# A fused recurrence and rational-activation kernel: last unit's denominator sum by accumulating DMA, and a new order table

## The chip, the cores and the metric

The kernel runs on one core of a Trainium2 chip. The metric is the device time of one execution in microseconds; the time before is 221.01 us, the median of 5 runs (220.28 to 221.08). A profile of one further execution shows every engine's instructions: PE (matrix multiply), DVE (elementwise), ACT (activations), POOL (here small copies and the issue of DMAs that cast or accumulate), SP (issue of plain DMAs). All times inside an execution are counted from its first instruction.

## The reference

Two parts follow each other. The first is a gated linear recurrence per batch and head (4 x 8, 768 steps, 48 channels); the second feeds the result, as 3072 tokens of 384 channels, through a projection to 2048, a rational function, and a projection back to 384.

```python
f = 1.0 / (1.0 + np.exp(-f_logit))
for t in range(S):
    state = f[:, :, t, :, None] * state + np.einsum('bhd,bhe->bhde', k[:, :, t], v[:, :, t])
    y[:, :, t] = np.einsum('bhd,bhde->bhe', q[:, :, t], state)
x = np.ascontiguousarray(attn_out.transpose(0, 2, 1, 3)).reshape(B * S, H * D)
h = x @ w_in
h2 = h * h
P = a[0] + a[1] * h + a[2] * h2 + a[3] * h2 * h
Q = 1.0 + np.abs(b[0]) * np.abs(h) + np.abs(b[1]) * h2
g = P / (Q + 1e-06)
out = g @ w_out
```

## The kernel before

The work is cut into 12 units: unit n is batch n mod 4 and one third of the sequence, 256 tokens, held as two chunks of 128. The recurrence is done in chunked form, with a state carried from third to third of a batch, so unit n needs unit n−4. Each unit goes through some 70 *steps*. A step is a small Python function that records one instruction, or a group on one engine.

The whole program is one table, `ORDER`, a text of 829 steps such as `h 3 4 8 @2`: name, unit, further numbers (first and last of 16 blocks of 128 hidden channels, or of 4 head pairs, or a chunk), and `@` with the PSUM slot that it takes. Scheduling is manual (`tc.manual_schedule()`): the program is recorded in the table's order, so each engine runs its own steps in that order, strictly one after another; waits between engines, and waits for a buffer or a slot to come free, are put in automatically. There are four PSUM slots of one buffer each. A step that waits holds up everything behind it on its engine, and for SP and POOL everything behind it in their DMA queues.

Steps that matter here, by engine:

- SP: `ld n f|k|q` load a unit's gate logits, keys and queries in f32 (L200, 384 KB; unit 0 in two halves), in three rotating buffers; `ld 0 v` too. `ab_` loads the coefficients `b` and `a`, each spread over 128 partitions (L228, L230). `so` stores a unit's output (L590).
- POOL: `ca`, `cb` make triangular masks and the identity; `wi` loads `w_in` with a cast (L216), `wo` `w_out` (L220), `ld n v` the values (L200), `vm` copies some of their columns (L388). `ta` (L559) and `zd` (L525) are DMAs within on-chip memory that add 512 KB of bf16 onto another tile.
- ACT: `ef`, `ls` make the log of the gate (L308, L313); `A n 1|0` exponentials of its running sum (L332); `ae` those of the sum over the unit (L461); `ye` evicts the recurrence's output, scaled (L456); `hy` evicts the projection (L488), `sa` its square (L496); `ln` and `lz` take the logarithm of the denominator (L516 from PSUM, L532 from on-chip memory); `ex` its exponential with sign turned, that is the reciprocal (L540); `oe`, `oc` evict the output. `b1_` issues a DMA that loads `b` onto one partition (L224), and `rg` loads two registers from coefficients made of it.
- DVE: `cz`, `cc` fill constants; `hv` writes a word of `w_in`'s tile, so that `wi` can't start earlier; `fa 0` and `fa 1` make coefficients from `b` on one and on 128 partitions (L277 to L287), `fb` scales `a` with them (L296); `xa n 1|0` multiply keys or queries by `A` (L337); `Te` copies transposes out of PSUM (L356); `mk` masks the scores (L377); `st` forms the new state (L465); `sq` squares (L492), `ab` takes the absolute value (L500), `p1`, `p2`, `pm` and `tv` build the numerator (L545, L550, L555, L563), `gm` multiplies by the reciprocal (L568).
- PE: `cs` running sums (L323), `T` transposes (L348), `sc` scores (L369), `sv` and `id` the state (L413, L424), `yb` the recurrence's output (L394), `h` first projection (L474), `u` a sum by two identity matmuls (L508), `o` second projection (L581).

The denominator of a unit is `z = |h| + h2`, with the coefficients folded into scales. It is summed in one of two ways. Either PE adds the two tiles into PSUM, and the logarithm reads PSUM, in steps of 4 blocks:

```python
for x, src in ((0, s["h2"]), (1, s["z"])):
    for m in range(m0, m1, 2):
        nc.tensor.matmul(t[:, m - m0:m - m0 + 2, :].rearrange("p m t -> p (m t)"), ident,
                         fl(src, m, m + 2), start=(x == 0), stop=(x == 1))
```

or `zd` adds them by DMA, and `lz` reads the sum from on-chip memory in one step of 8 blocks:

```python
nc.gpsimd.dma_start(out=fl(s["z"], m0, m1), in_=fl(s["h2"], m0, m1), accum_op=ALU.add)
```

Units 0 and 1 use PE throughout, units 2 to 10 use `zd` for one half or both, unit 11 uses PE for all of its four quarters. At the start of the table, DVE's steps are `cz 0; cc; cz 1; fa 0; cz 3; cz 2`, the four `xa 0` with `hv 0` after two of them, `Te 0` in two halves, `st 0 0`, two `mk 0`, `xa 1 1; st 0 1; fa 1; xa 1 0; fb; Te 1`. PE's in that stretch are `yb 0; id 1 0; h 0 0 4; T 1; h 0 4 8; sc 1 0; sc 1 1`.

Of the kernel before, what the change touches and what calls it, by code (L numbers as in the profile page):

```python
# [19 lines left out]
b1_; cz 0; cb; ca; ld 0 f 2 4; ld 0 f 0 2; ld 0 q 2 4; cc; ld 0 k 2 4; cz 1; ld 0 k 0 2; fa 0  # L20
ef 0 2 4; ld 0 q 0 2; ls 0 2 4; ef 0 0 2; cs 0 2 4 @0; ld 0 v; cz 3; ls 0 0 2; A 0 1 2 4; ld 1 f
cs 0 0 2 @1; cz 2; A 0 0 2 4; A 0 1 0 2; xa 0 1 2 4; A 0 0 0 2; ld 1 k; xa 0 0 2 4; rg; hv 0
xa 0 1 0 2; T 0 2 4 @1; wi 0 4; ld 1 q; xa 0 0 0 2; id 0 0 @0; Te 0 2 4; T 0 0 2 @2; vc 0; ab_
wi 4 8; vm 0 0 s; Te 0 0 2; ae 0; sc 0 0 @2; sc 0 1 @1; sv 0; ef 1; ld 2 f; ld 1 v; ls 1; st 0 0
wi 8 16; mk 0 1; id 0 1; vm 0 1 s; cs 1 @3; mk 0 0; A 1 1; yb 0 0 4 @2; A 1 0; xa 1 1; st 0 1
id 1 0 @3; ye 0; fa 1; ld 2 q; h 0 0 4 @2; ld 2 k; xa 1 0; fb; T 1 @0; hy 0 0 4; h 0 4 8 @1; ae 1
Te 1; sc 1 0 @0; hy 0 4 8; sc 1 1 @2; mk 1 0; ld 3 f; ef 2; sv 1; vm 1 0; sq 0 0 8; ls 2; ld 2 v
cs 2 @0; ab 0 0 8; ld 3 v; mk 1 1; u 0 0 4 @1; A 2 1; vm 1 1; A 2 0; st 1 0; u 0 4 8 @2; p1 0 0 8
ln 0 0 4; id 1 1; h 0 8 12 @0; p2 0 0 8; ld 3 q; ln 0 4 8; pm 0 0 8; yb 1 0 4 @2; ex 0 0 8; xa 2 0
h 0 12 16 @1; st 1 1; ld 3 k; ye 1; tv 0 0 8; hy 0 8 12; h 1 4 8 @2; xa 2 1; hy 0 12 16; vm 2 0  # L30
id 2 0 @0; gm 0 0 8; wo 8 12; hy 1 4 8; sv 2; ld 4 f; vm 2 1; h 1 0 4 @1; sq 0 8 16; ae 2; sa 1 4 8
wo 0 4; wo 4 8; ef 3; p1 0 8 16; h 1 12 16 @2; wo 12 16; hy 1 0 4; st 2 0; ab 0 8 16; vm 3 1; id 2 1
ld 4 q; sa 1 0 4; T 2 @3; ab 1 0 8; vm 3 0; ld 4 v; st 2 1; ls 3; u 1 0 4 @1; Te 2; hy 1 12 16
cs 3 @0; pm 0 8 16; ln 1 0 4; u 0 12 16 @3; A 3 1; sc 2 0 @2; p2 0 8 16; h 1 8 12 @1; A 3 0; mk 2 0
ln 0 12 16; sc 2 1 @0; xa 3 1; u 0 8 12 @2; ld 5 f; hy 1 8 12; ld 4 k; mk 2 1; u 1 4 8 @3; ef 4
id 3 0 @1; ln 0 8 12; ab 1 8 16; yb 2 0 4 @0; xa 3 0; ls 4; sv 3; ld 5 v; p1 1 0 16; ye 2; T 3 @2
ln 1 4 8; o 0 0 0 4 @0; Te 3; ex 0 8 16; cs 4 @3; o 0 1 0 4; tv 0 8 16; h 2 0 4 @2; A 4 0; sq 1 8 16
A 4 1; o 0 1 4 8; sa 2 0 4; gm 0 8 16; h 2 4 8 @3; ld 6 f; ae 3; ld 5 q; hy 2 0 4; pm 1 8 16
o 0 1 8 12; hy 2 4 8; h 2 12 16 @2; pm 1 0 8; ex 1 0 8; st 3 0; o 0 0 4 8; p2 1 0 16; id 3 1
o 0 1 12 16; hy 2 12 16; o 0 0 8 12; st 3 1; ta 1 0 8; sa 2 4 8; xa 4 1; sc 3 0 @1; sc 3 1 @2  # L40
vm 4 1; o 0 0 12 16; ef 5; ld 7 f; mk 3 0; ld 5 k; h 2 8 12 @3; ef 6; mk 3 1; ld 6 q; oe 0 0 2 s
u 1 8 12 @1; hy 2 8 12; ab 2 0 8; yb 3 0 4 @2; xa 4 0; ls 5; u 1 12 16 @3; vm 5 1; ab 2 8 16
ln 1 8 12; vm 4 0; sq 2 8 16; T 4 @0; zd 2 0 8; ln 1 12 16; so 0 0 2; cs 5 @1; ta 1 8 16; ye 3; Te 4
u 2 12 16 @3; A 5 0; p1 2 0 16; sv 4 @0; A 5 1; sc 4 1 @2; ex 1 8 16; h 3 0 4 @1; mk 4 1; ld 6 k
p2 2 0 16; h 3 4 8 @2; hy 3 0 4; gm 1 0 8; ln 2 12 16; id 4 0; u 2 8 12 @1; ae 4; hy 3 4 8; xa 5 0
h 3 12 16 @3; ls 6; st 4 0; xa 5 1; ef 7; id 4 1; ld 8 f; h 3 8 12 @2; st 4 1; hy 3 12 16; pm 2 0 8
sv 5 @0; ln 2 8 12; sc 4 0 @3; id 5 0; ta 2 0 8; hy 3 8 12; mk 4 0; o 1 0 0 4 @1; ae 5; o 1 0 4 8
lz 2 0 8; st 5 0; cs 6 @3; ab 3 0 8; pm 2 8 16; o 1 1 0 4; A 6 0; yb 4 0 4 @2; gm 1 8 16; ta 2 8 16
A 6 1; id 5 1; o 1 1 4 8; ex 2 0 8; sq 3 0 8; o 1 0 8 12; o 1 1 8 12; p1 3 0 16; zd 3 0 8; ye 4
T 5 @3; ld 6 v; ex 2 8 16; st 5 1; h 4 0 4 @2; Te 5; ld 7 v; ld 9 f; ld 7 k; o 1 0 12 16; vm 5 0  # L50
pm 3 0 8; ld 7 q; hy 4 0 4; h 4 4 8 @3; sa 4 0 4; xa 6 0; o 1 1 12 16; ab 3 8 16; sa 4 4 8
h 4 8 12 @2; gm 2 0 8; hy 4 4 8; sq 3 8 16; h 4 12 16 @0; oe 1 0 2 s; hy 4 8 12; gm 2 8 16
o 2 0 0 4 @1; hy 4 12 16; sc 5 0 @2; xa 6 1; sc 5 1 @3; o 2 0 4 8; ls 7; mk 5 0; o 2 1 0 4; lz 3 0 8
cs 7 @0; ab 4 0 8; ld 10 f; u 3 8 12 @2; so 1 0 2; mk 5 1; A 7 1; o 2 1 4 8; ln 3 8 12; p2 3 0 16
yb 5 0 4 @3; A 7 0; sv 6 @2; ab 4 8 16; ld 8 k; ta 3 0 8; ye 5; o 2 0 8 12; pm 3 8 16; ex 3 0 8
# [12 lines left out]
sc 7 0 @2; hy 6 0 4; o 4 0 0 4 @1; mk 7 0; sa 6 0 4; o 4 1 0 4; o 4 0 4 8; mk 7 1; ex 5 8 16; T 8 @3
sq 6 8 16; yb 7 0 4 @0; ls 9; p1 6 0 16; u 6 12 16 @2; ld 10 v; ye 7; lz 5 0 8; o 4 1 4 8; ab 6 0 8
Te 8; o 4 1 8 12; h 7 4 8 @0; ln 6 12 16; pm 6 8 16; ex 5 0 8; h 7 0 4 @3; gm 5 8 16; vm 9 0  # L70
ld 10 q; zd 6 0 8; ld 10 k; o 4 0 8 12; p2 6 0 16; so 3 0 2; hy 7 4 8; o 4 0 12 16; vm 9 1; cs 9 @2
hy 7 0 4; gm 5 0 8; ta 6 8 16; sc 8 1 @0; A 9 0; o 4 1 12 16; sq 7 0 8; A 9 1; h 7 12 16 @3; mk 8 1
oe 4 0 2 s; ef 10; sc 8 0 @2; ld 11 q; sv 8 @1; pm 6 0 8; id 8 0; hy 7 12 16; u 6 8 12 @0; mk 8 0
ls 10; ta 6 0 8; h 7 8 12 @3; ae 8; ln 6 8 12; xa 9 1; cs 10 @2; hy 7 8 12; st 8 0; o 5 0 0 4 @0
ab 7 0 8; ex 6 8 16; yb 8 0 4 @3; xa 9 0; zd 7 0 8; sv 9 @1; sq 7 8 16; id 9 0; ye 8; o 5 1 0 4
p1 7 0 16; ae 9; A 10 0; o 5 1 4 8; ef 11; T 9 @3; st 9 0; ld 11 k; ab 7 8 16; A 10 1; h 8 12 16 @1
Te 9; zd 7 8 16; lz 6 0 8; h 8 8 12 @2; pm 7 8 16; hy 8 12 16; xa 10 1; o 5 0 4 8; hy 8 8 12
sc 9 1 @3; p2 7 0 16; sc 9 0 @1; o 5 1 8 12; so 4 0 2; ls 11; h 8 4 8 @2; mk 9 0; ex 6 0 8
ta 7 8 16; ld 11 v; mk 9 1; o 5 0 8 12; o 5 1 12 16; hy 8 4 8; ab 8 8 16; o 5 0 12 16; sa 8 4 8
# [565 lines left out]
```

## Time and profile before

| what | us |
|---|---|
| median of 5 runs | 221.01 |
| the profiled execution's own time | 220.79 |
| its span, first to last instruction | 219.1 |
| `hy` on ACT, 48 of 128x1024 | 49.3 |
| `ex` on ACT, 23 of 128x2048 | 44.8 |
| `lz` on ACT, 13 of 128x2048, mean 1996 ns | 25.7 |
| `ln` on ACT, 22 of 128x1024, mean 1077 ns | 23.3 |
| `u` on PE, the 74 recorded matmuls of 128x512, mean 379 ns | 23.2 |
| POOL issuing 13 `zd`, mean 1100 ns | 14.2 |
| a `zd` from issue to landing, median | 6.3 |
| a `ta` from issue to landing, median | 6.4 |

The page gives the busy time of each engine, and for a group of instructions the summed and the mean duration. Consecutive instructions of one engine overlap a little, so durations add up to somewhat more than the time that passes; where it matters, start-to-start distances in the timeline are the better measure. The time of an execution is 1.7 us longer than the span. Idle time before an instruction is shown in brackets, with what ended it.

### The profile page before, as it was taken

To read this page: it belongs to the slowest core of one execution; us is meant where nothing else is said; L and a number is where in the kernel's file an instruction comes from. 1 tells how busy PE (TensorE), PEld (TensorE's weight loads), DVE (VectorE), ACT (ScalarE), POOL (GpSimd) and SP (SyncE) were. 2 spreads that over 40 slices of the span, in tenths; PEclk is the share of its full clock that TensorE was granted. 3 is DMA by queue.
4 is the path that set the end of the run, shared out by engine and by line. 5 is a ranking of instruction groups with operands and counts; after the bars stand their busy time and mean duration, and the time that the engine had idled before them with its cause. 6 is when DMAs were issued, how large, how long until landed. Compare 5 with 4: busy or idle time off the path is not lost.

```text
span 219.1 us, 7100 instructions
## 1 busy us (share of the span) xinstructions
PE 202.4 (92%) x3106; PEld 143.4 (65%) x3120; DVE 202.9 (93%) x249; ACT 200.4 (91%) x215; POOL 78.7 (36%) x95
## 2 busy tenths in 40 slices
PE   1679699999999999999999999999999999999991
PEld 1446378567757778577668676786867776865450
DVE  4766999999999999999999999999999999999951
ACT  5563699999999999999999999999999999999980
POOL 4570529020261149362916633123423323231000
PEclk9999999999999999999999999999999999999999
DMA  6999999999899899699999999967988998999515
GB/s 154 292 199 202 225 225 212 204 210 242 211 227 240 222 208 152 126 274 191 214 246 257 213 269 203 212 129 130 191 155 156 195 203 165 187 200 190 107 45 144
DMA packets 62128, 42.86 MB, mean 196 GB/s; under 512 B 51474, under 2 KB 57362, under 8 KB 62098
## 3 DMA queue, kind: packets, MB, share of 16 engines
q0 software_dynamic: 19792, 23.14, 64.4%
q1 hardware_dynamic: 42144, 19.08, 34.5%
q8 instruction: 24, 0.39, 0.7%
q10 hardware_dynamic: 162, 0.20, 0.3%
q14 instruction: 6, 0.05, 0.1%
HBM read 25.17 MB, written 4.72 MB: 136 GB/s over the span
## 4 chain that ended last, share of the span: by engine, by line
PE 40%; ACT 29%; DVE 16%; issue 6%; DMA 4%; SPq 4%; ACTq 0%; DVEq 0%
PE hp L474 14%; PE op L581 13%; ACT qi L540 7%; ACT hy L488 6%; DMA b<-in_moe_b_dram 4%; SPq L200 4%; ACT lq L516 3%; ACT A L332 3%; ACT h L496 3%; PE u L508 3%; DVE h L492 3%; PE y L394 2%; PE tp L348 2%; ACT lq L532 2%; DVE gall L568 2%
## 5 line engine op out<-in xcount | busy, mean ns | idle before, releaser
L474 PE MATMUL hp<-xT,w_in_sb 128*128 128x256 bf16 x576 | 70.3, 276 | 0.8 <-ACT xT L456 0.3
L581 PE MATMUL op<-w_out_sb,gall 128*128 128x384 bf16 x384 | 69.9, 326 | 0.0
L474 PEld LDWEIGHTS <-w_in_sb 128*128 128x128 bf16 x576 | 56.1, 99 | 11.6 <-issue 1.4
L488 ACT CAST hy<-hp 128x1024 bf16<-128x1024 f32 x48 | 49.3, 1072 | 4.4 <-PE hp L474 4.4
L581 PEld LDWEIGHTS <-gall 128*128 128x128 bf16 x384 | 36.2, 98 | 23.4 <-DVE gall L568 1.1
L540 ACT ACTIVATE qi<-lq 128x2048 bf16<-128x2048 f32 (+1 forms) x25 | 46.8, 1899 | 0.1
L559 POOL DMA_DIRECT2D gall<-hy x21 | 20.1, 959 | 65.5 <-DVE gall L555 18.7
L388 POOL COPY vmp<-vn 128x128 bf16<-128x128 bf16 x22 | 27.4, 1257 | 15.9 <-DMA vn<-in_v_dram 12.6
L568 DVE TENSOR_TENSOR gall<-gall,qi 128x2048 bf16<-128x2048 bf16 (+1 forms) x25 | 29.5, 1178 | 1.5 <-ACT qi L540 1.3
L377 DVE TENSOR_TENSOR scm<-sc,mask 128x1024 bf16<-128x1024 f32 x24 | 28.8, 1216 | 0.6 <-PE sc L369 0.5
L555 DVE TENSOR_TENSOR gall<-gall,h 128x2048 bf16<-128x2048 bf16 (+1 forms) x25 | 29.2, 1172 | 0.0
L532 ACT ACTIVATE lq<-z 128x2048 f32<-128x2048 bf16 x13 | 25.7, 1996 | 0.0
L516 ACT ACTIVATE lq<-u 128x1024 f32<-128x1024 f32 x22 | 23.3, 1077 | 0.0
L525 POOL DMA_DIRECT2D z<-h x13 | 14.2, 1100 | 20.9 <-DVE z L500 4.7
L332 ACT ACTIVATE A<-cs 128x768 f32<-128x768 f32 (+1 forms) x26 | 19.2, 794 | 2.7 <-PE cs L323 2.6
L492 DVE TENSOR_TENSOR h<-hy 128x2048 bf16<-128x2048 bf16 (+1 forms) x18 | 20.9, 1163 | 0.0
L323 PE MATMUL cs<-lsp,Ui 128*128 128x384 bf16 (+1 forms) x39 | 11.1, 346 | 6.7 <-ACT lsp L313 6.7
L200 POOL DMA_DIRECT2D vn<-in_v_dram x11 | 12.0, 1093 | 14.7 <-issue 13.8
L500 DVE TENSOR_SCALAR z<-hy 128x2048 uint16<-128x2048 uint16 (+1 forms) x25 | 17.0, 681 | 0.0
L550 DVE TENSOR_SCALAR hy<-hy,a_sb 128x4096 bf16<-128x4096 bf16 (+2 forms) x15 | 16.8, 1126 | 0.1
L545 DVE TENSOR_SCALAR gall<-hy,a_sb 128x4096 bf16<-128x4096 bf16 (+2 forms) x15 | 16.9, 1124 | 0.0
L356 DVE COPY qkT<-tp 128x2048 bf16<-128x2048 bf16 (+1 forms) x13 | 14.8, 1135 | 1.6 <-PE tp L348 1.6
(70 smaller groups left out, 265.8 us busy)
## 6 DMA issues: line engine op xcount, KB each, us to landing
gall<-hy POOLq DMA_DIRECT2D x21, 512.0 KB, 6.4
z<-h POOLq DMA_DIRECT2D x13, 512.0 KB, 6.3
fn<-in_f_logit_dram SPq DMA_DIRECT2D x11, 384.0 KB, 8.3
kn<-in_k_dram SPq DMA_DIRECT2D x11, 384.0 KB, 6.4
qn<-in_q_dram SPq DMA_DIRECT2D x11, 384.0 KB, 10.7
out_dram<-osb SPq DMA_DIRECT2D x22, 192.0 KB, 3.7
vn<-in_v_dram POOLq DMA_DIRECT2D x11, 192.0 KB, 9.3
w_out_sb<-in_moe_w_out_dram POOLq DMA_DIRECT2D x4, 384.0 KB, 9.3
```

What stands on the lines that cost most here:

```text
L332: nc.scalar.activation(t, src, AF.Exp, scale=1.0 if x else -1.0)
L377: nc.vector.tensor_mul(t, s["sc", g].rearrange("s r a i t -> s (r a) (i t)"), mb)
L388: nc.gpsimd.tensor_copy(dst, src)
L474: nc.tensor.matmul(t[:, m - m0, :].rearrange("f (j t) -> f j t", j=UB), w_in_sb[:, kk, m * P:(m + 1) * P], s["x"][:, :, kk, :], start=(kk ...
L488: nc.scalar.copy(fl(big(s, "hy", "hy", 3), m0, m1), fl(s["hp", m0], 0, m1 - m0))
L492: nc.vector.tensor_mul(fl(big(s, "h2", "h2", 2), m0, m1), fl(s["hy"], m0, m1), fl(s["hy"], m0, m1))
L516: nc.scalar.activation(fl(s["lq", g], m0 - 8 * g, m1 - 8 * g), fl(s["u", m0], 0, m1 - m0), AF.Ln, scale=rsig2, bias=1.0 + 1e-6)
L532: nc.scalar.activation(fl(s["lq", g], m0 - 8 * g, m1 - 8 * g), fl(s["z"], m0, m1), AF.Ln, scale=rsig2, bias=1.0 + 1e-6)
L540: nc.scalar.activation(fl(s["qi", g], m0 - 8 * g, m1 - 8 * g), fl(s["lq", g], m0 - 8 * g, m1 - 8 * g), AF.Exp, scale=-1.0)
L555: nc.vector.tensor_mul(fl(s["g"], m0, m1), fl(s["g"], m0, m1), fl(s["h2"], m0, m1))
L568: nc.vector.tensor_mul(fl(s["g"], m0, m1), fl(s["g"], m0, m1), fl(s["qi", g], m0 - 8 * g, m1 - 8 * g))
L581: nc.tensor.matmul(s["op", j][:, 0:DM], s["g"][:, m, C * j:C * j + C], w_out_sb[:, m, :], start=(m == 0), stop=(m == KF - 1))
```

## The change

For the first half (blocks 0 to 8) of the last unit's denominator, `u 11 4 8`, `u 11 0 4`, `ln 11 4 8` and `ln 11 0 4` go, and `zd 11 0 8` and `lz 11 0 8` come in. All other steps stay, 827 in all, but the table is a new one: on each engine the steps stand in another order, near the former one. In PE's order the furthest step moves by 15 places (of 258), in ACT's by 19 (of 217), in DVE's by 8 (of 221), in POOL's by 8, in SP's by 6. Slots (`@`) are dealt anew as well.

Moves that stand out: `ca` before `cb`; `cz 0` behind the other `cz` and `cc`; `b1_` from the front of ACT's order to behind `ls 0 0 2`; `fa 0` from before the `xa 0` to behind all four; `hv 0` after three of them instead of two; `st 0 0` behind both `mk 0`; `fa 1` ahead of both `xa 1`; `T 1` ahead of `h 0 0 4`; `sv 0` ahead of `sc 0`; `ef 3` ahead of `A 2`; `ld 3 f`, `ld 4 f`, `ld 5 f` and `ld 7 f` earlier among the loads; `ef 9`, `ef 10` and `ef 11` earlier by 11, 16 and 19 places; `ld 8 k`, `ld 8 q` ahead of `so 0`.

The first and the last lines of the table, as a diff:

```diff
 ORDER = """
-b1_; cz 0; cb; ca; ld 0 f 2 4; ld 0 f 0 2; ld 0 q 2 4; cc; ld 0 k 2 4; cz 1; ld 0 k 0 2; fa 0
-ef 0 2 4; ld 0 q 0 2; ls 0 2 4; ef 0 0 2; cs 0 2 4 @0; ld 0 v; cz 3; ls 0 0 2; A 0 1 2 4; ld 1 f
-cs 0 0 2 @1; cz 2; A 0 0 2 4; A 0 1 0 2; xa 0 1 2 4; A 0 0 0 2; ld 1 k; xa 0 0 2 4; rg; hv 0
-xa 0 1 0 2; T 0 2 4 @1; wi 0 4; ld 1 q; xa 0 0 0 2; id 0 0 @0; Te 0 2 4; T 0 0 2 @2; vc 0; ab_
-wi 4 8; vm 0 0 s; Te 0 0 2; ae 0; sc 0 0 @2; sc 0 1 @1; sv 0; ef 1; ld 2 f; ld 1 v; ls 1; st 0 0
-wi 8 16; mk 0 1; id 0 1; vm 0 1 s; cs 1 @3; mk 0 0; A 1 1; yb 0 0 4 @2; A 1 0; xa 1 1; st 0 1
-id 1 0 @3; ye 0; fa 1; ld 2 q; h 0 0 4 @2; ld 2 k; xa 1 0; fb; T 1 @0; hy 0 0 4; h 0 4 8 @1; ae 1
-Te 1; sc 1 0 @0; hy 0 4 8; sc 1 1 @2; mk 1 0; ld 3 f; ef 2; sv 1; vm 1 0; sq 0 0 8; ls 2; ld 2 v
+cz 2; ca; ld 0 f 2 4; ld 0 f 0 2; ld 0 q 2 4; cb; cc; cz 1; ld 0 k 2 4; cz 3; ld 0 k 0 2; ef 0 2 4
+cz 0; ld 0 q 0 2; ls 0 2 4; ld 0 v; ef 0 0 2; cs 0 2 4 @0; ls 0 0 2; ld 1 f; b1_; cs 0 0 2 @1
+ld 1 q; A 0 1 2 4; A 0 0 2 4; xa 0 1 2 4; A 0 1 0 2; A 0 0 0 2; xa 0 1 0 2; ld 1 k; xa 0 0 0 2; hv 0
+xa 0 0 2 4; T 0 0 2 @1; wi 0 4; fa 0; vc 0; ab_; T 0 2 4 @0; vm 0 1 s; vm 0 0 s; Te 0 0 2; id 0 0 @2
+rg; ld 2 f; Te 0 2 4; wi 4 8; sv 0; ae 0; ef 1; sc 0 1 @0; ld 3 f; sc 0 0 @1; ls 1; mk 0 1; ld 2 k
+ld 1 v; id 1 0 @3; mk 0 0; cs 1 @0; wi 8 16; st 0 0; fa 1; A 1 0; id 0 1; yb 0 0 4 @1; A 1 1; xa 1 0
+ye 0; xa 1 1; ld 2 q; st 0 1; T 1 @1; fb; h 0 0 4 @2; Te 1; ld 4 f; sc 1 0 @1; hy 0 0 4; h 0 4 8 @0
+mk 1 0; ef 2; sc 1 1 @1; ae 1; hy 0 4 8; mk 1 1; ls 2; sq 0 0 8; vm 1 1; cs 2 @1; vm 1 0; ef 3; sv 1
...
-sq 11 0 8; o 9 1 0 4; hy 11 8 12; o 9 0 4 8; p1 11 0 8; ex 10 0 8; o 9 1 4 8; gm 9 8 16; u 11 4 8 @2
-pm 11 0 8; o 9 0 8 12; oe 8 0 2 s; o 9 1 8 12; hy 11 12 16; p1 11 8 12; so 8 0 2; o 9 0 12 16
-p2 11 0 8; lz 10 8 16; o 9 1 12 16; gm 10 0 8; ta 11 0 8; u 11 0 4 @3; sq 11 12 16; o 10 0 0 4 @1
-ln 11 4 8; ab 11 12 16; o 10 1 0 4; sq 11 8 12; ex 10 8 16; p1 11 12 16; o 10 1 4 8; ab 11 8 12
-u 11 12 16 @2; p2 11 8 12; p2 11 12 16; ln 11 0 4; o 10 0 4 8; pm 11 8 12; oe 9 0 2 s; gm 10 8 16
...
+gm 8 8 16; ta 10 0 8; h 11 8 12 @3; lz 10 0 8; ab 11 0 8; o 8 1 8 12; sq 11 0 8; o 8 1 12 16
+ex 9 8 16; o 8 0 8 12; gm 9 0 8; zd 11 0 8; o 8 0 12 16; pm 10 8 16; o 9 0 0 4 @1; oe 8 0 2 s
+h 11 12 16 @0; ex 10 0 8; p1 11 0 8; ta 10 8 16; so 8 0 2; gm 9 8 16; o 9 0 4 8; o 9 1 0 4
+hy 11 12 16; p2 11 0 8; o 9 1 4 8; gm 10 0 8; lz 10 8 16; o 9 1 8 12; o 9 0 8 12; pm 11 0 8
+o 9 1 12 16; hy 11 8 12; p1 11 12 16; o 10 0 0 4 @0; ta 11 0 8; sq 11 12 16; ex 10 8 16; o 10 0 4 8
+ab 11 8 12; o 10 1 0 4; ab 11 12 16; p1 11 8 12; o 10 1 4 8; p2 11 12 16; lz 11 0 8; o 9 0 12 16
+sq 11 8 12; gm 10 8 16; u 11 12 16 @3; u 11 8 12 @2; oe 9 0 2 s; p2 11 8 12; pm 11 12 16; ex 11 0 8
...
```

Between them every line of the table differs in the same manner: steps exchanged with neighbours, none added or taken out.

## The prediction

> **What bounds the kernel now.** First the page's busy times and the windows: where is there idle time to win?
>
> ```profile
> PE 202.4 (92%) x3106; PEld 143.4 (65%) x3120; DVE 202.9 (93%) x249; ACT 200.4 (91%) x215; POOL 78.7 (36%) x95
> ...
> 0.00:15.00 15.00, 7.26 (x102) 5.06 (x102) 9.68 (x36) 8.35 (x16) 8.62 (x23) 1.00 0.96 217
> 15.00:30.00 15.00, 12.27 (x221) 8.40 (x226) 11.96 (x23) 9.31 (x13) 4.39 (x7) 1.00 1.30 211
> 30.00:120.00 90.00, 88.65 (x1481) 64.22 (x1488) 89.69 (x95) 89.71 (x99) 38.59 (x35) 1.00 1.09 215
> 120.00:205.00 85.00, 84.70 (x1261) 60.94 (x1263) 84.91 (x89) 84.98 (x81) 27.11 (x32) 1.00 0.97 187
> 205.00:219.10 14.10, 9.50 (x54) 4.83 (x52) 6.69 (x10) 8.06 (x10) 0.00 (x0) 0.98 0.32 84
> ```
>
> Columns of a window: length, busy us of PE, PEld, DVE, ACT, POOL, granted clock, DMA share, GB/s. From 30 to 205 us DVE and ACT are idle 0.4 and 0.3 us of 175: no order can win much there, and neither engine's work changes. Idle time lies ahead of 30 us (ACT 12.3, DVE 8.4) and behind 205. So a shift of the moment at which the three engines become full goes nearly whole into the time. What sets that moment shows the DVE timeline:
>
> ```profile
> 15.50 0.96 DVE L337 TENSOR_TENSOR qkp<-kn,A 128x768 bf16<-128x768 f32 x1 [0.43 <-ACT A L332]
> 16.37 0.55 DVE L465 TENSOR_TENSOR state<-sv,alast 128x384 bf16<-128x384 f32 x1
> 18.20 0.17 DVE L277 TENSOR_SCALAR bm<-b 128x2 uint32<-128x2 uint32 x1 [1.28 <-DMA b<-in_moe_b_dram]
> ...
> 19.35 0.96 DVE L337 TENSOR_TENSOR qkp<-qn,A 128x768 bf16<-128x768 f32 x1
> 20.23 0.74 DVE L296 TENSOR_SCALAR a_sb<-a_sb,sig 128x3 f32<-128x3 f32 x3
> 21.49 1.23 DVE L356 COPY qkT<-tp 128x2048 bf16<-128x2048 bf16 x1 [0.53 <-PE tp L348]
> ```
>
> `fa 1` (L277 to L285) waits for the broadcast load of `b`; behind it stand `xa 1 0`, `T 1`, `Te 1`. Two steps, `xa 1 1` and `st 0 1`, run before that wait. PE meanwhile does `h 0 0 4`:
>
> ```profile
> 17.55 2.72 PE L474 MATMUL hp<-xT,w_in_sb 128*128 128x256 bf16 x12 [0.31 <-ACT xT L456]
> 20.37 1.08 PE L348 MATMUL tp<-ident,qkp 128*128 128x128 bf16 x16
> 21.29 1.48 PE L474 MATMUL hp<-xT,w_in_sb 128*128 128x256 bf16 x12
> ```
>
> The first twelve matmuls of `h` start 0.214 us apart, the next twelve 0.109; the first `T` (7.43) starts its transposes 0.107 apart, `T 1` 0.056. PE runs at half speed until about 20.3, with a granted clock of 1.00 in these windows, so that column doesn't show it.
>
> Last the end of the chain of waits:
>
> ```profile
> 205.46 1.02 PE u L508 x4
> ...
> 206.52 6.87 PE op L581 x40
> ...
> 213.41 0.33 ACT osb L604
> ```
>
> **The change at the start of the program.** Times below go by start-to-start distances in the timeline.
>
> *The wait for b moves ahead of more work.* In the new order `fa 1` stands before both `xa 1`, and `T 1` before `h 0 0 4` on PE. Let L be the landing of `b`. From L: `fa 1` 1.15 (18.20 to 19.35); two `xa` of 0.87, 1.75; `T 1` on a PE idle since `yb 0` (about 16.7), hence slow, 16 x 0.107 and 0.15 to drain, 1.86 — ends L+4.8. `h 0 0 4`, 12 x 0.214 = 2.57, ends L+7.3. `sc 1 0`, 0.3, then `h 0 4 8` at full speed 12 x 0.109 and 0.15, ends L+9.1; `sc 1 1` 0.25; `mk 1 1` 1.13, ends L+10.5 (`mk 1 0` lies in the shadow of `h 0 4 8`). Behind it DVE is full: `sq` 1.13, `ab` 0.60, `p1` 0.72, `st` 0.47: L+13.5. Before, DVE has done the same twelve steps at 28.6 (`p2 0 0 8` starts at 28.64). So DVE is late by **L − 15.1**. ACT agrees: it waits from `ye 0` (about 17) for `h 0 0 4` and for `u`.
>
> *Where L goes.* Before, the load is issued at 9.62 and lands at 18.18. Of its 128 packets of 8 bytes 120 start between 13.84 and 15.87, the last eight, one DMA engine's share, between 17.40 and 17.69; that engine carried an instruction fetch of 0.94 us at 16.04. What holds the SP queue (q1) up is w_in from POOL (q0): q1 moves 821 packets in 9 to 10 us, and once q0 has begun
>
> ```profile
> q0 software_dynamic: 150, 0.13, 93.4%
> q1 hardware_dynamic: 97, 0.04, 19.1%
> ```
>
> (11 to 12 us; packets, MB, share), on average about 320 per us from 10 to 14. w_in waits for `hv 0`, which ran at 7.33. Now `hv 0` comes after three `xa` instead of two, the third with its `q` landed at 7.45: first `xa` 6.28 (`k` landed 6.23), second 6.95 (third `A` ends about 6.9), third 7.48 to 7.97, so `hv` about 0.6 late. q1 gains some (821 − 320) x 0.6 = 300 packets, 1 us of its contended rate. Then the slow engine's share starts at 17.40 − 0.94 − 1.0 = 15.5, ahead of the fetch, and lands 0.5 later: L = 16.0. If it still falls behind the fetch, 17.2; if nothing is gained, 18.2. I take 16.5: late by **+1.4**; ends: 14.7 (when DVE is ready for it, −0.4) and 18.2 (+3.1).
>
> *`b1_` after `ls 0 0 2`, `fa 0` after the first `xa`.* Its issue took 0.54 and its one packet started 0.9 us after the issue began; issued at about 5.1 it lands by about 8, when `xa` ends (8.5). `fa 0` (1.35, from 3.82 to 5.17 before) now stands ahead of `Te 0`, which ends at 11.2 instead of 10.6. `st 0 0` behind the two `mk` gives it back: the second `mk` ends at 14.2 (15.06 before), `yb 0` starts at 15.2 (15.12). The rest of DVE is idle until L anyway: 0. Without that cover: +0.6.
>
> A rule speaks against the placing of `T 1`. The Trainium skill ("TensorE: Matmul & The Clock Gate", Part 1) says the PE gets its full clock only after some 3.4 us of activity in a free-running window, and Part 4 that transposes don't count for it. Our row agrees with the first (`yb 0` at 15.12, full speed from 20.37); no row shows the second. By it `T 1` warms nothing, `sc 1 0` and a part of `h 0 4 8` stay slow too, and the sum would be up to 0.8 us higher.
>
> **Loads.** On SP, `ld 3 f` overtakes `ld 2 k` and `ld 2 q`, `ld 4 f`, `5 f`, `7 f` overtake others. A load lands as late as its place in the queue: the load that stood where `ld 3 f` stands now landed at 27.3 (`ef 3` wants it at about 27), the next at 29.4 (`xa 2 1`: 33, as before), the one after at 32.5 (`xa 2 0`, now behind `gm 0 0 8`, which ended at 35.2). `ld 8 k` and `ld 8 q` before `so 0` hold that store until unit 5's `xa` are done; its buffer is wanted only at `oe 2`. `ld 9 f` moves behind `ld 9 q`, and `ef 9` up by 11 places: by the distances of the ACT and DVE rows it lands at about 98 and is used at about 106. On POOL, `wo` issues some 6 us earlier but queues behind the same `vn` loads. All about 0; ends 0 and +0.7 (a late `ef 3`).
>
> **The middle.** A new order on all engines: 0.7 us is the whole idle time to win; a loss is open. I take +0.2, ends −0.5 and +1.5.
>
> **The end.** Two `u` go: 8 x 0.215 = 1.7 us of PE at 197 and 201. Two `ln` (904 ns start to start) go for one `lz` (1800): ACT ±0. One `zd`: 0.86 us of POOL, 512 KB, landed in 4.6 to 7.1 us from 140 us on; between `hy 11 4 8` and `lz 11 0 8` stand eight ACT steps, 11.5 us; `ab` and `sq` with the DVE steps ahead of them take 3 to 5 of these, the transfer up to 7.5 with its issue: it fits, barely at the worst. `ta 10 8 16` and `ta 11 0 8` queue behind it on POOL for 0.9 us; `gm 11 0 8` waits for the latter, with 2 us of slack before. PE's relief is worth little: after the last `gm` (211.81 to 212.50) 12 matmuls x 0.163 must follow, which ends at 214.45 against about 214.7 before. So −0.2; ends −0.3 and +1.0 (`zd` late).
>
> **Sum** against the profiled execution's own 220.79 (span 219.1 and 1.7 around it): 220.79 + 1.4 + 0.2 − 0.2 = 222.2. The median is 0.2 above that execution, so **222.4**.
>
> **Rivals.** (1) `b` doesn't gain: it lands at 18.2 as before, because the instruction fetch still sits in its way; +3.1: 224.1. For it: 8 of 128 packets decide; against it: the later `hv`. Chance 0.24. (2) `b` lands by 15.2, before DVE asks for it, and the start costs nothing; with −0.5 in the middle and −0.3 at the end: 220.2 (faster). It decides from L = 15.1 downward; 120 of 128 packets were nearly there before. Chance 0.20. (3) `b` lands at 15.4: the start costs 0.3, the end gives 0.2 back: 221.1, no change. Chance 0.13. (4) The added transfer is late: `lz 11 0 8` waits 1 us for `zd`, which two transfers in flight can bring about; on top of the forecast 223.4. Chance 0.08. The forecast keeps 0.35.
>
> Changes under 0.2% (0.44 us) can't be told from none here. Slower: forecast, (1), (4) = 0.67; same 0.13; faster 0.20. Range for 8 in 10: 220.3 (rival 2) to 224.3 (rival 1); forecast alone 221.6 to 223.1 (L from 16.0 to 17.2, rounded outward).
>
> **What would show it.** In the changed profile: `fa 1`'s L277 row on 128 partitions with its wait on `b`, its start = L; `T 1`'s row with about 1.9 us and `h 0 0 4` behind it with about 2.6; `sq 0 0 8` (L492) starting at L+10.5; POOL's first w_in row at about 8.3 instead of 7.71; DVE and ACT full from there to 205; in the tail ACT's `lz 11 0 8` without a wait on `z`. Wrong if `b` lands before 15, if the PE is at full speed in `h 0 0 4`, or if ACT and DVE show over 1 us of idle time between 40 and 205.

## The result, and the profile after

The changed kernel takes 222.73 us (median of 46 runs, 220.06 to 226.65) against 220.84 for the kernel before (88 runs beside them, 219.41 to 224.45). The ratio is 1.0067, 95% interval 1.0052 to 1.0081: slower by 1.1 to 1.8 us. It is nearer to 1 than the ratio of the two medians, because ratios here leave out executions in a slow state (more than 1.5% above the fastest of their kernel), and the medians don't. The profiled execution took 222.37 us, 1.58 us more than that of before, with a span of 220.6.

The page's busy times, and the windows with the same columns as before:

```profile
PE 202.5 (92%) x3097; PEld 143.7 (65%) x3112; DVE 204.0 (92%) x249; ACT 200.6 (91%) x214; POOL 74.3 (34%) x96
...
0.00:15.00 15.00, 7.96 (x111) 5.43 (x111) 10.23 (x37) 8.37 (x16) 8.34 (x22) 1.00 0.90 215
15.00:30.00 15.00, 12.22 (x269) 8.44 (x269) 11.80 (x21) 9.59 (x13) 6.27 (x10) 1.00 1.27 223
30.00:120.00 90.00, 88.64 (x1435) 64.35 (x1430) 89.90 (x95) 89.73 (x100) 30.72 (x30) 1.00 1.13 213
120.00:205.00 85.00, 82.83 (x1247) 59.74 (x1248) 83.75 (x86) 83.57 (x79) 29.00 (x34) 1.00 0.98 186
205.00:220.60 15.60, 10.85 (x63) 5.79 (x61) 8.37 (x13) 9.30 (x10) 0.00 (x0) 0.99 0.49 117
```

Read it by ACT (the fourth pair), whose work is the same in both kernels: 200.4 and 200.6 us. By 30 us it has done 17.96 us of it, 0.30 more than before. Between 120 and 205, where it was idle for 0.02 us, it is now idle for 1.43. So the loss isn't where the prediction put most of it. The DVE timeline at the start says the same:

```profile
14.82 0.17 DVE L277 TENSOR_SCALAR bm<-b 128x2 uint32<-128x2 uint32 x1
...
19.52 1.23 DVE L356 COPY qkT<-tp 128x2048 bf16<-128x2048 bf16 x1 [0.60 <-PE tp L348]
22.57 1.22 DVE L377 TENSOR_TENSOR scm<-sc,mask 128x1024 bf16<-128x1024 f32 x1 [1.83 <-PE sc L369]
...
25.47 1.22 DVE L492 TENSOR_TENSOR h<-hy 128x2048 bf16<-128x2048 bf16 x1
```

`fa 1` starts at 14.82 without a wait: `b` landed at 14.79, not at 16.5. Behind it PE is slow, as predicted; its timeline:

```profile
17.61 1.87 PE L348 MATMUL tp<-ident,qkp 128*128 128x128 bf16 x16 [0.94 <-ACT xT L456]
19.27 2.77 PE L474 MATMUL hp<-xT,w_in_sb 128*128 128x256 bf16 x12
```

`sq 0 0 8` at 25.47 is L + 10.7 (predicted L + 10.5), and the twelve DVE steps are done at 28.74, against 28.64 in the profile of before.

What is new is one wait in the middle, here in the PE and ACT timelines:

```profile
145.71 0.41 PE L369 MATMUL sc<-qkT 48*64 48x128 bf16 x13
147.17 0.25 PE L369 MATMUL sc<-qkT 48*64 48x128 bf16 x3 [1.05 <-issue]
```

```profile
150.18 1.02 ACT L496 ACTIVATE h<-hp 128x1024 bf16<-128x1024 f32 x1 [1.08 <-PE hp L474]
```

PE stops inside `sc 9 1`, 13 matmuls in, and waits 1.05 us for nothing that the profile can name ("issue"). And the chain of waits now ends otherwise. Before, PE's `u` and `o` stood in it from 205 on; now an adding DMA does:

```profile
198.25 8.60 DMA gall<-hy
...
206.94 1.24 DVE gall L568
...
208.22 6.73 PE op L581 x40
```

That is `ta 10 8 16`, for which `gm 10 8 16` waits 0.89 us; behind it `gm 11 0 8` waits 0.35 for `ta 11 0 8`.

### The profile page after: what moved, and what is told of

The parts are those of the page before. It is cut to its first block, busy times and chain, and to the rows that moved or that the text cites. A ratio compares the mean times of both kernels' runs of the same rounds, so it can differ in the third digit from the quotient of the medians.

```text
span 220.6 us, 7080 instructions
## 1 busy us (share of the span) xinstructions
PE 202.5 (92%) x3097; PEld 143.7 (65%) x3112; DVE 204.0 (92%) x249; ACT 200.6 (91%) x214; POOL 74.3 (34%) x96
## 3 DMA queue, kind: packets, MB, share of 16 engines
HBM read 25.17 MB, written 4.72 MB: 135 GB/s over the span
## 4 chain that ended last, share of the span: by engine, by line
ACT 47%; DVE 21%; PE 16%; issue 9%; DMA 5%; ACTq 0%; DVEq 0%
ACT hy L488 11%; ACT qi L540 9%; PE op L581 6%; ACT lq L516 6%; ACT h L496 5%; PE hp L474 4%; ACT A L332 4%; DMA gall<-hy 4%; DVE scm L377 4%; DVE gall L555 4%; ACT lsp L313 3%; ACT fn L308 2%; DVE gall L568 2%; ACT lq L532 2%; PE y L394 2%
## 5 line engine op out<-in xcount | busy, mean ns | idle before, releaser
L581 PE MATMUL op<-w_out_sb,gall 128*128 128x384 bf16 x384 | 68.7, 326 | 0.4 <-DVE gall L568 0.3
L488 ACT CAST hy<-hp 128x1024 bf16<-128x1024 f32 x48 | 49.9, 1075 | 4.9 <-PE hp L474 4.8
L540 ACT ACTIVATE qi<-lq 128x2048 bf16<-128x2048 f32 (+1 forms) x25 | 47.6, 1930 | 0.0
L559 POOL DMA_DIRECT2D gall<-hy x21 | 20.7, 1002 | 75.4 <-issue 25.6
L532 ACT ACTIVATE lq<-z 128x2048 f32<-128x2048 bf16 x14 | 27.3, 1961 | 0.0
L388 POOL COPY vmp<-vn 128x128 bf16<-128x128 bf16 x22 | 20.7, 1056 | 8.1 <-DMA vn<-in_v_dram 8.1
L516 ACT ACTIVATE lq<-u 128x1024 f32<-128x1024 f32 x20 | 22.0, 1131 | 0.1
L348 PE MATMUL tp<-ident,qkp 128*128 128x128 bf16 x192 | 14.3, 234 | 2.7 <-DVE w_in_sb L210 1.8
L496 ACT ACTIVATE h<-hp 128x1024 bf16<-128x1024 f32 x14 | 15.4, 1101 | 1.1 <-PE hp L474 1.1
```

The lines of the kernel that those rows point to most:

```text
L488: nc.scalar.copy(fl(big(s, "hy", "hy", 3), m0, m1), fl(s["hp", m0], 0, m1 - m0))
L496: nc.scalar.activation(fl(big(s, "h2", "h2", 2), m0, m1), fl(s["hp", m0], 0, m1 - m0), AF.Square)
L516: nc.scalar.activation(fl(s["lq", g], m0 - 8 * g, m1 - 8 * g), fl(s["u", m0], 0, m1 - m0), AF.Ln, scale=rsig2, bias=1.0 + 1e-6)
L532: nc.scalar.activation(fl(s["lq", g], m0 - 8 * g, m1 - 8 * g), fl(s["z"], m0, m1), AF.Ln, scale=rsig2, bias=1.0 + 1e-6)
L540: nc.scalar.activation(fl(s["qi", g], m0 - 8 * g, m1 - 8 * g), fl(s["lq", g], m0 - 8 * g, m1 - 8 * g), AF.Exp, scale=-1.0)
L581: nc.tensor.matmul(s["op", j][:, 0:DM], s["g"][:, m, C * j:C * j + C], w_out_sb[:, m, :], start=(m == 0), stop=(m == KF - 1))
```

## The experiments

Twelve kernels, in three groups, each timed in five rounds beside the kernel before, which read 220.9, 220.77 and 220.65 us in the three groups.

### First group: which half of the change costs

`e1_sum_alone` keeps the former order and makes only the exchange of the sum:

```diff
-u 11 4 8; u 11 0 4; ln 11 4 8; ln 11 0 4
+zd 11 0 8 (POOL, behind ta 10 8 16); lz 11 0 8 (ACT, where ln 11 0 4 stood)
```

> The former table with the sum of the last unit's first half by zd and lz alone; DVE's order stays the former one, and zd stands behind ta 10 8 16 on POOL. Theory A (the time is lost behind 120 us by the new order: a PE stall of 1.05 us near 146 without a data wait, and accumulating DMAs that land late at the end): no change, -0.3 to +0.3 us. Rival B (the start costs it, as predicted): no change either. Rival C (the added transfer is what costs): +1.5 us.

Measured: 222.51 us, ratio 1.0079 (1.0050 to 1.0109). The DMA alone costs as much as the whole change. Its ACT timeline shows the fourth rival's wait, on `zd`:

```profile
205.12 1.91 ACT L532 ACTIVATE lq<-z 128x2048 f32<-128x2048 bf16 x1 [1.15 <-DMA z<-h]
```

`e2_order_alone` keeps the new order and takes the exchange back (the two `u` behind `o 9 1 4 8` and `o 9 1 12 16` on PE, a place that I chose):

```diff
-zd 11 0 8; lz 11 0 8
+u 11 4 8; u 11 0 4; ln 11 4 8; ln 11 0 4
```

> The new table with the two u and the two ln put back in place of zd and lz; DVE's order is the new one throughout. Theory A: +1.2 to +1.7 us against before. Rival B: +1.5. Rival C: no change, -0.3 to +0.3.

Measured: 224.26 us, ratio 1.0162 (1.0122 to 1.0202). The PE stall is there (1.35 us at 147.52); in the tail ACT waits 1.14 us for PE at 208.28, and DVE 2.29 us for ACT at 210.92.

`e3_new_start` and `e4_old_start` exchange the first 175 steps (up to about 45 us):

```diff
 e3: steps 1 to 175 of the new table, then the former order with u and ln
 e4: steps 1 to 175 of the former table, then the new order with zd and lz
```

> The first 175 steps of the new table (some 45 us), then the rest of the former table, with u and ln. Theory A: -0.5 to +0.4 us, since the start of the changed kernel's profile has DVE through the same twelve steps at 28.75 us where before has 28.64. Rival B: +1.4. Rival C: 0.

> The first 175 steps of the former table, then the rest of the new one, with zd and lz. Theory A: +1.2 to +1.7 us. Rival B: +0.1. Rival C: +1.5.

Measured: e3 221.72 us, 1.0044 (1.0015 to 1.0073); e4 223.52 us, 1.0126 (1.0086 to 1.0167). Both lose something at the seam (in e3 0.94 us of DVE at 48.7; in e4 0.77 of ACT and 0.80 of DVE at 48), so their ratios are likely too high. e4 is 0.6%, some 1.3 us, above the changed kernel, of which about 0.8 us stand at its seam; what is left is within the intervals, so e4 doesn't settle what the new start is worth in time. The parts don't add, which none of the theories foresaw: in the former order the DMA costs 0.8%, in the new one the changed kernel is 0.9% below e2, which lacks the DMA. In this group the PE stall of 1.05 us shows up in both runs with the new rest (1.35 in e2, 0.84 in e4) and in neither with the former one; e3 has another, 0.69 us at 115.89.

### Second group: the stall, and the landing of b

Where does PE's stall come from? The instruction queue (q8) moves 24 blocks of 16 KB in an execution, for some 6220 recorded PE instructions: one block for about 259. In the eight stalls of this study PE resumes 1.22 to 1.46 us after such a block has landed:

```
run        block lands   PE resumes   lag    idle
after      145.86        147.17       1.31   1.05
e2         146.21        147.52       1.32   1.35
e3         114.49        115.89       1.40   0.69
e4         147.09        148.31       1.22   0.84
f4         145.87        147.34       1.46   1.12
g2         144.97        146.26       1.29   0.74
g3         147.91        149.30       1.39   0.26
g4         146.51        147.91       1.40   0.97
```

Why the block comes late shows in the windows of the changed kernel (columns: length, busy PE, clock, DMA share, GB/s):

```profile
140.00:142.00 2.00, 1.72 (x82) 1.00 1.06 214
142.00:144.00 2.00, 2.00 (x76) 1.00 1.06 210
144.00:146.00 2.00, 2.00 (x36) 1.00 0.41 67
```

The DMA engines are full until 144, with `ta 6 0 8` and `ta 6 8 16`, issued 0.54 us apart (136.43 and 136.97, landed 143.68 and 146.38), and the block starts at 144.89, in the stretch where the share falls. Before, 142 to 144 had a DMA share of 0.43, and the block started at 143.08.

`f1_adds_apart` moves the second of the two adding DMAs, on POOL:

```diff
-zd 6 0 8; ta 6 0 8; ta 6 8 16; ld 11 v; zd 7 8 16
+zd 6 0 8; ta 6 0 8; ld 11 v; ta 6 8 16; zd 7 8 16
```

> The changed kernel with one POOL step moved: the accumulating DMA ta 6 8 16, issued 0.54 us behind ta 6 0 8 (136.97 and 136.43 us), now stands behind ld 11 v, about 8 us later. Theory A (the PE stall of 1.05 us at 147 is late instructions: the 16-KB instruction fetch started at 144.89 only, right behind four microseconds in which the accumulating DMAs filled the DMA engines; in the kernel before it started at 143.08): the fetch starts by about 143.3, the stall inside sc 9 1 is under 0.3 us, ACT's 1.08 us at 150 goes, and the time falls by 0.5 to 1.0 us, to 221.7 to 222.2. Rival B (PE stalls because of the burst of small matmuls itself, whatever the DMAs do): stall of about 1 us at the same instruction, time 222.7. Rival C (the stall is real, but the tail takes it up, since DVE waits there for ta 10 8 16 anyway): stall gone, time 222.4 to 222.8.

`f2_scores_behind_h` leaves the DMAs and moves the place where PE ran out:

```diff
-h 8 8 12 @0; sc 9 1 @3; h 8 12 16 @2
+h 8 8 12 @0; h 8 12 16 @2; sc 9 1 @3
```

> The changed kernel with one PE step moved: sc 9 1 behind h 8 12 16, so that some 26 wide matmuls and weight loads stand ahead of the place where PE ran out. Theory A (late instructions): the fetch starts as late as before (about 144.9), but PE reaches the end of what it has about 2.8 us later, so the stall is under 0.3 us; the time falls by 0.5 to 1.0 us, to 221.7 to 222.2. Rival B (the burst): stall at sc 9 1 gone too if the wide matmuls break the burst up; this run tells A from B only together with the run that moves the DMA. Rival C (the tail takes it up): stall gone, time 222.4 to 222.8.

Measured: f1 222.18 us, 1.0034 (0.9997 to 1.0072); f2 221.81 us, 1.0050 (1.0022 to 1.0077). The stall is gone from both. In f1 the block started at 142.17, and PE goes through `sc 9 1` in one piece. Windows of f1 as above, then its PE timeline:

```profile
140.00:142.00 2.00, 1.72 (x107) 1.00 0.66 131
142.00:144.00 2.00, 2.00 (x31) 1.00 0.06 12
```

```profile
145.25 0.42 PE L369 MATMUL sc<-qkT 48*64 48x128 bf16 x16
145.60 2.79 PE L474 MATMUL hp<-xT,w_in_sb 128*128 128x256 bf16 x24
```

In f2 the block landed at 144.37 (f2 ran ahead here, so it came earlier than expected), and PE got to the place in question at 146.0 only. So theory A stands, and B (the burst itself) falls with f1, which has the same burst. That the stall goes is shown by the traces; what the time gains by it is not clear of the noise: by the ratios 0.4 to 0.7 us of 1.05, and their intervals overlap that of the changed kernel. In the tail of f2 DVE waits longer for the same DMA, 2.08 us instead of 0.89; its timeline:

```profile
206.10 1.23 DVE L568 TENSOR_TENSOR gall<-gall,qi 128x2048 bf16<-128x2048 bf16 x1 [2.08 <-DMA gall<-hy]
```

`ta 10 8 16` was issued 2.04 us earlier than in the changed kernel (196.21 for 198.25) and landed 0.85 earlier (206.00 for 206.85), 9.79 us after its issue. Rival C holds in part.

`f3_before_hold_later` and `f4_hold_earlier` test the prediction's largest term, the landing L of `b`:

```diff
 f3, in the kernel before:
-xa 0 0 2 4; rg; hv 0; xa 0 1 0 2
+xa 0 0 2 4; rg; xa 0 1 0 2; hv 0
 f4, in the changed kernel:
-xa 0 1 0 2; ld 1 k; xa 0 0 0 2; hv 0
+xa 0 1 0 2; hv 0; ld 1 k; xa 0 0 0 2
```

> The kernel before with one DVE step moved: hv 0, which holds the w_in load back, stands behind three xa instead of two, as in the changed kernel. By the prediction's step (w_in's packets hold up the small load of b, so a later hold brings b's landing L forward): L goes from 18.2 to 14.8 to 16.5, DVE's wait of 1.28 us ahead of fa 1 shrinks to under 0.4, and the time falls by 0.3 to 1.0 us, to 219.9 to 220.6. Rival (L was moved by something else in the new order, b1_, the SP order or the phase of the instruction fetch): L stays at about 18, time 220.9 within 0.3.

> The changed kernel with hv 0 moved back behind two xa, as in the kernel before. By the prediction's formula (the start costs L - 15.1): L goes from 14.8 back to about 18, the start then costs about 3 us, and the time is 224.7 to 225.8. Rival (L was moved by something else): L stays at about 15, time 222.4 to 222.9. Third way (L goes back, but the formula overstates what hangs on it): L about 18, time under 224.

Measured: f3 220.69 us, 0.9986 (0.9961 to 1.0011), no change; f4 222.76 us, 1.0097 (1.0060 to 1.0135). In f3 `hv 0` ran at 7.84 instead of 7.33, and L is 14.70 instead of the 18.18 in the profile of before. That looks like the prediction's step, but it isn't evidence for it: e1 and e4 begin with the former start, their hold isn't moved (7.42 and 7.51), and their L is 14.66 and 14.52. So an L near 14.6 comes without a later hold as well, and the 18.18 was one execution's. The DVE timeline of f3, then that of e1:

```profile
16.88 0.16 DVE L277 TENSOR_SCALAR bm<-b 128x2 uint32<-128x2 uint32 x1
...
21.90 1.23 DVE L356 COPY qkT<-tp 128x2048 bf16<-128x2048 bf16 x1 [2.26 <-PE tp L348]
```

```profile
16.94 0.18 DVE L277 TENSOR_SCALAR bm<-b 128x2 uint32<-128x2 uint32 x1
...
22.01 1.23 DVE L356 COPY qkT<-tp 128x2048 bf16<-128x2048 bf16 x1 [2.29 <-PE tp L348]
```

In both, the 1.28 us of waiting for `b` are absent, and DVE waits 2.26 and 2.29 us for `T 1` instead, which stands behind `h 0 0 4` on PE. `Te 1` comes 0.41 later in f3 than in the profile of before: its `T 1` started 0.26 us earlier (20.11 for 20.37) and ran 0.67 longer (1.75 for 1.08). In f4 the hold went back by only 0.35 us (8.01 to 7.66, since the first `xa` ends later there), and L was 15.36. The expectation of 3 us rested on L going back to 18, and L was near 18 in the profile of before alone: in the other thirteen profiles of this study it lies between 13.74 and 15.42.

### Third group: the tail, and a slow PE at the start

`g1_stall_and_tail` adds to f2 an edit of the tail; `g2_tail_alone` makes that edit in the changed kernel:

```diff
-gm 8 8 16; ta 10 0 8; ... ab 11 0 8; sq 11 0 8; gm 9 0 8; zd 11 0 8; pm 10 8 16; ... ta 10 8 16
+gm 8 8 16; pm 10 8 16; ta 10 8 16; ta 10 0 8; ... ab 11 0 8; sq 11 0 8; gm 9 0 8; zd 11 0 8
```

> The changed kernel with two edits: sc 9 1 behind h 8 12 16 on PE (which took the stall away in the run before), and on DVE pm 10 8 16 ahead of ab 11 0 8 and sq 11 0 8, with the accumulating DMA ta 10 8 16 ahead of zd 11 0 8 on POOL. In the run with the first edit alone DVE waited 2.08 us at 206.10 for ta 10 8 16, issued at 196.21 and landed at 206.00, and PE 1.53 us at 207.38 behind it: what the missing stall gave came back there. Theory A (the loss of the changed kernel is these two things, the instruction stall and the late add of unit 10, and the second hides the first): ta 10 8 16 is issued about 3 us earlier and lands before 203, DVE's and PE's waits go under 0.5 us, the time falls to 220.0 to 221.0, no worse than before. Rival B (zd 11 0 8, now issued about 1 us later, makes lz 11 0 8 wait on ACT instead): ACT waits up to 2 us at 204, time 221.5 to 222.5. Rival C (loss spread over the start and many small places): time about 221.8, as with the first edit alone.

> The changed kernel with the tail edit alone (pm 10 8 16 ahead of ab 11 0 8 and sq 11 0 8, ta 10 8 16 ahead of zd 11 0 8); sc 9 1 where it was. Theory A: the PE stall of about 1 us stays at 147, DVE's 0.89 and 0.35 us of waits at 207 and 209.6 go, the time falls by 0.3 to 0.9 us, to 221.8 to 222.4; the two edits together then gain more than the sum of each alone, since each alone leaves the other's wait. Rival B (lz 11 0 8 waits for zd instead): no gain, 222.5 to 223.2.

Measured: g1 224.95 us, 1.0201 (1.0165 to 1.0236); g2 225.30 us, 1.0259 (1.0213 to 1.0304). Much worse. As made, the edit put `ta 10 8 16` also ahead of `ta 10 0 8`, which the expectation didn't say, and `gm 10 0 8` needs that one first. In g1 three adding DMAs of 512 KB were issued within 1.64 us (194.31, 194.84, 195.95) and landed after 4.64, 8.32 and 10.60 us. The DVE timeline, then the ACT timeline of g1:

```profile
203.25 1.23 DVE L568 TENSOR_TENSOR gall<-gall,qi 128x2048 bf16<-128x2048 bf16 x1 [4.12 <-DMA gall<-hy]
```

```profile
206.57 1.91 ACT L532 ACTIVATE lq<-z 128x2048 f32<-128x2048 bf16 x1 [2.26 <-DMA z<-h]
```

So these two runs don't say what a cured tail would give. They do show the three transfers sharing the DMA engines (DMA share 0.92, 1.05 and 0.88 in 195 to 200, 200 to 203 and 203 to 206): they landed at 198.95, 203.16 and 206.55, 4.2 and 3.4 us after one another. The order `ta 10 0 8`, `ta 10 8 16`, `zd 11 0 8` wasn't tried.

`g3_h_first` puts `h 0 0 4` ahead of `T 1` in g1; `g4_warm` adds five matmuls that nothing reads:

```diff
 g3:
-T 1 @1; h 0 0 4 @2; sc 1 0 @1; h 0 4 8 @0; sc 1 1 @1
+h 0 0 4 @1; T 1 @2; h 0 4 8 @0; sc 1 0 @2; sc 1 1 @1
 g4, on top:
+zw; wm 3 @3 (behind cs 0 0 2); wm 2 @0 (behind yb 0)
```

> The kernel with both edits, and besides h 0 0 4 ahead of T 1 and h 0 4 8 ahead of sc 1 0 on PE, as in the kernel before (slots exchanged to suit). The prediction's start step put T 1 ahead of h 0 0 4 on a slow PE: T 1 took 1.87 us and h 0 0 4 2.77 us there. Theory A (that order costs DVE and ACT what the early b gives): hy 0 0 4 starts at about 20.3 instead of 22.07, sq 0 0 8 (L492) at 24.3 to 24.9 instead of 25.47, and the time falls by 0.3 to 0.9 us against the run with both edits. Rival (the order of T 1 and h only exchanges what waits: Te 1 then comes 2 us later, and unit 1's scores with it): sq 0 0 8 at 25 or later, time within 0.3 us of the run with both edits.

> As the run with h 0 0 4 first, with five more matmuls of 128x512 zeros on PE that nothing reads: three ahead of the first transposes (PE is idle there for 1.8 us), two between yb 0 and h 0 0 4 (idle 0.9 us); DVE clears the zeros in about 0.1 us. The prediction took PE to run at half speed until it had been busy for long enough. If that is so, and these fill enough: h 0 0 4's twelve matmuls start 0.109 apart instead of 0.214 from some point on, its row is under 2.2 us instead of 2.7, and the time falls by up to 0.6 us against the run without them. Rival (they are too few, or what counts is something else): h 0 0 4 stays at 2.7 us, time within 0.3 us.

Measured: g3 226.29 us, 1.0252 (1.0220 to 1.0284); g4 225.73 us, 1.0228 (1.0191 to 1.0265). In g3 `hy 0 0 4` came at 20.49, as expected, but `sq 0 0 8` at 26.66: PE was slow for longer, `T 1` took 1.91 us and `h 0 4 8` 2.04. In g4 the extra matmuls worked at the place meant: PE rows

```profile
17.85 1.98 PE L474 MATMUL hp<-xT,w_in_sb 128*128 128x256 bf16 x12
19.67 1.06 PE L348 MATMUL tp<-ident,qkp 128*128 128x128 bf16 x16
```

and `sq 0 0 8` at 25.17, 1.5 us ahead of g3. The times of g3 and g4 can't be told apart, with the tail of g1 behind both. g4 shows one thing more: its stall (0.97 us) came at the ninth matmul of `h 8 12 16`, whereas that of g3, the same order without the ten added PE instructions, came at the second of `sc 9 1`, before it; counted from the start of the program it is the same place, the 4536th recorded PE instruction, as it is in f4 and g2. In e3 it is the 3499th, in the changed kernel the 4522nd, four blocks apart (1023 instructions). (Some records are missing in each trace, up to about 15 in the changed kernel, e2 and e4, so that these counts are good to about as much.)

## Why the prediction was right, and where it was wrong

The number was right, 222.4 for 222.73, and its sum of 222.2 for the profiled execution met 222.37. Its terms weren't: the loss that the start was to bring didn't come, and the middle and the end brought one of the same size. That the number met the measurement is luck.

**Start, +1.4: wrong.** Part of the mechanism held: behind `b`, `T 1` and `h 0 0 4` ran slow (1.87 and 2.77 us for 1.86 and about 2.6), and DVE's work followed the formula to 0.45 us (its terms add up to L + 13.4, where it says 13.5). Two things failed. L was mis-sized: 14.79 for 16.5. The step is "q1 gains some (821 − 320) x 0.6 = 300 packets": from 10 to 11 us q1 moved 781 packets where it had moved 304 before, and the load was issued 0.88 us earlier as well (8.74 for 9.62), which the sum didn't count. And the base was one execution's: with the former start unchanged, e1 and e4 have L at 14.66 and 14.52, no wait for `b`, and a slow `T 1`. That a later hold brings `b` forward is therefore not shown. What does go with the hold is q1's share of that one microsecond: 304, 382, 495, 697 and 781 packets in before, e1, e4, f3 and the changed kernel, in the order of their holds. The first rival, `b` at 18.2 because of an instruction fetch, didn't come either; that a fetch was what held up its last eight packets before, no row shows, since none says which DMA engine carried it. From 11 to 12 us the two queues read, in the changed kernel (packets, MB, share of 16 engines):

```profile
q1 hardware_dynamic: 516, 0.19, 70.5%
q0 software_dynamic: 76, 0.07, 47.7%
```

There q1 holds its own, where it had moved 97 packets to q0's 150. That was the second rival's condition, given 0.20. But it holds with the former start too: q1 moved 511 and 490 packets there in e1 and e4, so the 97 is the odd one. By the formula the start then costs −0.3 us; by DVE's rows +0.1 against before, where the twelve steps were done at 28.64, and −0.3 to −0.4 against e1, e4 and f3, where they were done at 29.07, 29.13 and 29.05. And what the start is worth is not read from DVE alone. ACT's work done by 30 us is 17.96, 17.69, 18.44, 18.75, 18.95, 17.26, 18.18 and 18.37 us in the eight executions of the changed kernel, e2, e3, f1, f2, f4, g1 and g2, and 17.66, 17.14, 17.13 and 17.29 in before, e1, e4 and f3: on the mean 0.9 us more with the new start, though the two sets overlap. So the rows give no loss at the start, rather a gain; no run isolates it in the time.

**Middle, +0.2: too small,** though the end of +1.5 was given. The prediction's own mark for being wrong, over 1 us idle between 40 and 205, came true: 1.43 us on ACT and 1.32 on DVE, against 0.31 and 0.41 before (as did its other mark, `b` before 15). What it lacked is a resource: it priced the moved DMAs by who waits for their data, and PE's instructions use the same engines.

**End, −0.2: wrong.** The step that failed is "`ta 10 8 16` and `ta 11 0 8` queue behind it on POOL for 0.9 us". That is the time to issue; the 512 KB also take time on the DMA engines, which at the 192 to 202 GB/s of the full windows below is some 2.6 us (an estimate), and the engines were full. Windows of DVE of the kernel before, then of the changed one (last columns: clock, DMA share, GB/s):

```profile
195.00:200.00 5.00, 5.00 (x6) 1.00 1.01 192
200.00:206.00 6.00, 5.96 (x11) 1.00 0.74 160
```

```profile
195.00:200.00 5.00, 5.00 (x6) 1.00 1.01 202
200.00:206.00 6.00, 6.00 (x10) 1.00 1.01 194
```

`zd` itself landed at 202.05, in time for `lz 11 0 8` at 204.76, as forecast. But `ta 10 8 16`, which is on the chain, landed 4.6 us later than before (206.85 for 202.25), and most of that isn't the queue behind `zd`: it was issued 3.4 us later (198.25 for 194.85), and POOL had waited 1.18 us for `pm 10 8 16`, whose data it moves. On DVE `pm 10 8 16` came 3.64 us later, with `ab 11 0 8` and `sq 11 0 8` now ahead of it (1.73 us), and DVE was some 1.9 us late by then. The transfer itself took 1.2 us longer (8.60 for 7.40 us), with `zd` moving until 202.05. An earlier issue alone doesn't cure it: in f1 and f2 it was issued at 196.78 and 196.21 and landed at 206.64 and 206.00. The fourth rival had the right mechanism, a late transfer, at the wrong reader; in e1 it came true at the reader that it named.

ACT's idle time in the windows of the two profiles adds up to the loss: −0.30 us by 30, −0.02 from 30 to 120, +1.41 from 120 to 205, of which 1.08 is the wait behind PE's stall, +0.26 after that, and 0.17 us more of work: 1.5 in all, as the spans differ. This is one execution of each kernel, and the stall and the tail can't simply be added, as PE's last rows show, first of the kernel before, then of the changed one:

```profile
206.52 8.16 PE L581 MATMUL op<-w_out_sb,gall 128*128 128x384 bf16 x48
```

```profile
208.22 8.01 PE L581 MATMUL op<-w_out_sb,gall 128*128 128x384 bf16 x48 [0.34 <-DVE gall L568]
```

The last 48 matmuls start 1.70 us later, after only 0.34 us of waiting for the late DMA's reader. In f1 and f2, without the stall, that wait is 1.60 and 1.53 us, and they start at 208.02 and 207.38: the tail takes back most of what the stall gave. A version with both cured might gain about as much as that wait, some 1.5 us (an estimate); none was run. No run here beats the kernel before; f3 equals it.

## What to carry to other kernels

When a DMA is added or moved, price it on the DMA engines (bytes by the rate of that stretch, and the DMA share of the windows there), not only by the queue that issues it and the step that reads it: the one that comes late may be a neighbour, or the engine's own instructions. An engine that idles with no data to wait for may be out of instructions; compare where the blocks of the instruction queue land with where it resumes. Before a wait becomes a term of a sum, read it in more than one execution: the wait for `b`, on which most of this forecast rested, stood in the profile of before and not in e1 and e4, which have the same start. And a wait that goes, like the stall in f1 and f2, is worth only what the next one behind it leaves.

## What the runs showed of the hardware

PE resumed 1.22 to 1.46 us after its block of 16 KB had landed, in all eight stalls. Ahead of each, two adding DMAs of 512 KB had been issued 0.54 us apart, and in seven of the eight the block started as the DMA share fell; in e3 it started at 113.60 with the share still at 1.05 and the two in flight until 118.49 and 121.03. In f1, with the second of the two moved away, the block started at 142.17 instead of 144.89. That these DMAs delay it is shown by f1; that it always waits for their end is not, and when it was asked for, no row tells.

The moment at which PE goes to full speed at the start varies between executions of the same instructions. `h 0 0 4`, behind a first `T 1`, took 2.77, 2.77, 2.26, 2.13, 1.47, 2.41, 2.39 and 2.58 us in the changed kernel, e2, e3, f1, f2, f4, g1 and g2, with a granted clock of 1.00 in all of them; in the former order `T 1` took 1.08 us in the profile of before, and 1.81, 1.74 and 1.75 in e1, e4 and f3. So the prediction's "until about 20.3" was one draw: in e1, e4 and f3 a `T 1` that started about there still ran slow. Here f2's, the fastest draw:

```profile
17.94 1.17 PE L348 MATMUL tp<-ident,qkp 128*128 128x128 bf16 x16 [0.94 <-ACT xT L456]
18.95 1.47 PE L474 MATMUL hp<-xT,w_in_sb 128*128 128x256 bf16 x12
```

The Trainium skill ("TensorE: Matmul & The Clock Gate", Part 1) says that the activity window of 3.4 us runs freely, so that the point of change falls differently in each run. These rows agree that it differs, and by more than the 500 ns either way that the page gives: full speed is there before 18.95 in f2 and not before about 22 in the changed kernel. That transposes don't count (Part 4), no run here decides.
